# Scores of windowed attention on four quarters of the array, and value rows loaded with padding to 128 partitions

## The chip, the cores and the metric

The kernel runs on one core of a Trainium2 chip. Its engines work side by side: TensorE (PE in the profile, its weight loads PEld), VectorE (DVE), ScalarE (ACT), GpSimd (POOL) and SyncE (SP), which here only issues transfers. Transfers are carried by 16 DMA engines. The metric is the device time of one execution in microseconds (us); lower is better.

## The reference

Three stages follow one another: windowed attention, a routed mixture of experts with a skip score, and a second mixture of experts that fills each expert up to a capacity. The change is in the first one only:

```python
B, H, S, D = q.shape                       # 4, 8, 768, 64
block, window = (32, 16)
k_sum = k.reshape(B, H, nb, block, D).max(axis=3)     # nb = 24 block keys
v_sum = v.reshape(B, H, nb, block, D).mean(axis=3)    # 24 block values
scores_l = scale * np.matmul(q, k.transpose(0, 1, 3, 2))
mask_l = np.abs(pos[:, None] - pos[None, :]) < window
scores_s = scale * np.einsum('bhsd,bhnd->bhsn', q, k_sum) + np.log(block)
a = softmax(concat(where(mask_l, scores_l, -1e9), scores_s))
out = a @ concat(v, v_sum)
```

## The kernel before, in words

`phase_a` computes the attention and the gate logits of the first mixture. A *unit* is one batch and four heads (8 units, numbered 0 to 7); each unit is done in six *steps*, 48 in all. A step has four pairs of a head pair `h` and a window `w` of 64 queries; from unit 1 on these are two head pairs times the two windows 2t and 2t+1. A window sees 118 keys: 24 block keys and 94 neighbours. Queries and keys hold the 64 dims of two heads on the two halves of the 128 partitions.

Loop `i` runs over the steps, and the engines carry out their work in the order in which it is written there. In loop `i` TensorE gets:

- `qk(i)`, the scores: for each of the four pairs and each half `r` of the partitions, a product of 64 rows by 64 columns by 118 keys, written to the same half `r` of the PSUM tile `s_ps`. In float32 each product is two instructions of the trace, so 16 a step (L122). VectorE adds the mask and takes the maximum (L126).
- `ptr(i-2)`, four transposes (L137) of the exponentials that ScalarE made in loop `i-1` (`ex`, L132). ScalarE copies the result out (L139) ahead of the next `ex`.
- `pv(i-3)`, the products with the value rows (L148), 16 instructions: 118 rows by 64 columns by 65 (64 values and a column of ones for the sum). VectorE divides (L150 to L156).
- in the loops that follow odd units, `logits` (L172 to L177) and `post` (L162, L164): the gate's products and the transposes of the finished rows. The text calls these *post steps*.

So one step's scores run in the loop in which older steps are transposed and multiplied. The even window reads its keys from `kt`, the odd one from the copy `K2`, both of which ScalarE completes (L100, L103, L104) from the block maxima that VectorE takes (`prep_k`, L96).

Value rows: tile `VV` has, for each of the 12 windows, 24 rows of block means on partitions 0 to 23 and 96 rows of values on partitions 24 to 119. The values come by two DMAs a unit (L86) of 96 partitions; the ones of the mean rows are written once (L66). The means are made from a second copy of the values, `vt` (L84): POOL adds them up (`add_v`, L109), TensorE turns them (`turn_v`, L111), ScalarE scales them (L114), and POOL copies them into rows 0 to 23 (`mean_v`, L115). There are three `VV` tiles, used in turn.

`load(u)` issues a unit's transfers on the one SP queue, in this order: keys and queries of head pair 0, of head pair 1, `vt`, and the two of `VV`. Units 0 and 1 are issued at the start, unit `u+2` in the third step of unit `u`. SP waits where a buffer or a semaphore isn't free yet, and everything behind it waits too.

PSUM has eight banks: `s_ps`, `pt_ps` and `o_ps` with two buffers each, `xt_ps` and `l_ps` with one each.

After `phase_a` come the two mixtures, whose first weights are issued when the most loaded expert is known (late in `phase_a`).

Of the kernel before, what the change touches and what calls it, by code (L numbers as in the profile page):

```python
# [6 lines left out]
F32=mybir.dt.float32; BF=mybir.dt.bfloat16; F32R=mybir.dt.float32r; I32=mybir.dt.int32; U32=mybir.dt.uint32  # L7
AF=mybir.ActivationFunctionType; OP=mybir.AluOpType; AX=mybir.AxisListType
PSUM=bass.MemoryType.PSUM
B,H,S,D=4,8,768,64  # L10
N=B*S; DM=512; E=8; F=1024; CAP=384
NT=6
# [11 lines left out]
def layout(inp):  # L24
    q,k,v=inp['q'],inp['k'],inp['v']
    qd=np.ascontiguousarray(q.reshape(B,4,2,S,D).transpose(0,2,4,1,3)).reshape(B,128,4,S)
    kd=np.ascontiguousarray(k.reshape(B,4,2,S,D).transpose(0,2,4,1,3)).reshape(B,128,4,S)
    vd=np.ones((B,2,VR,4,65),np.float32)
    vd[:,:,:15]=0; vd[:,:,15+S:]=0
    vd[:,:,15:15+S,:,:64]=v.reshape(B,2,4,S,D).transpose(0,1,3,2,4)  # L30

    vd=vd.reshape(B,2,VR,260)[:,:,np.arange(VP)[:,None]+64*np.arange(12)[None,:]].reshape(B,2,VP,4,780)
    vd=np.concatenate([vd,np.zeros((B,2,VP,4,4),np.float32)],4)
    w17=np.concatenate([inp['moe_w_skip'][:,None],inp['moe_w_gate'],inp['moe2_w_gate']],1)
    w17=w17.reshape(4,128,17).transpose(1,0,2).reshape(128,68)
    w17=np.concatenate([w17,np.zeros((128,15),np.float32)],1)

    j=np.arange(94)[None,:]; c=np.arange(128)[:,None]%64
    band=(j>=c)&(j<=c+30)
    m=np.zeros((3,128,118),np.float32)  # L40
    m[:,:,:24]=np.float32(8*np.log(32))
    ok=[band&(j>=15), band, band&(j<=78)]
    for i in range(3): m[i,:,24:]=np.where(ok[i],0.0,NEG)
    cst=np.concatenate([m.transpose(1,0,2).reshape(128,354),np.eye(128,dtype=np.float32)],1).astype(np.float32)
    vt=np.ascontiguousarray(v.reshape(B,2,2,2,24,32,D).transpose(0,3,6,1,5,2,4)).reshape(B,128,2,1536)
    return dict(q=qd,k=kd,v65=vd,vt=vt,w17=w17,cst=np.ascontiguousarray(cst))

def phase_a(nc,tc,ctx,I,st):
    V=nc.vector; A=nc.scalar; T=nc.tensor; G=nc.gpsimd
    cl=ExitStack(); ld=cl.enter_context(tc.tile_pool(name="a_ld",bufs=2,side="right"))  # L50
    cp=ctx.enter_context(tc.tile_pool(name="a_const",bufs=1))
    wk=ctx.enter_context(tc.tile_pool(name="a_wk",bufs=3))
    ps=ctx.enter_context(tc.tile_pool(name="a_ps",bufs=2,space=PSUM))
# [3 lines left out]
    VV=[]; K2=[cp.tile([128,2,NT,118],F32,name=f"K2_{i}") for i in range(2)]  # L57

    wm=K2[1][:,0].rearrange("p a b->p (a b)")[:,0:256]; V.memset(wm,1.0); wm=wm.bitcast(BF)
    def spin(k,wm=wm):  # L60
        p=ps.tile([128,4,128],F32,name="s_ps").rearrange("p a b->p (a b)")
        for _ in range(k): T.matmul(p,wm[:,0:128] if len(wm.shape)==2 else wm[:,0,0:128],wm,start=True,stop=True)
    spin(WARM)
    for i in range(3):
        t=cp.tile([24+VP,12,4,65],F32,name=f"VV_{i}")
        G.memset(t[0:24,:,:,64:65],1.0); VV.append(t)  # L66
    KT=[]
    for i in range(3):
        t=ld.tile([128,2,864],F32,name=f"kt{i}",bufs=1)[:,:,25:25+KW]
# [7 lines left out]
    def load(u):  # L77
        b,g=units[u]
        kt=KT[u%3]; qd=ld.tile([128,2,S],F32,name="qd",bufs=3); vt=st["raw"].tile([128,2048],F32,name="wraw")
        vv=VV[u%3]; src=I['v65']  # L80
        def ld_k(h0,h1): nc.sync.dma_start(kt[:,h0:h1,39:39+S],I['k'][b,:,2*g+h0:2*g+h1,:])
        def ld_q(h0,h1): nc.sync.dma_start(qd[:,h0:h1],I['q'][b,:,2*g+h0:2*g+h1,:])
        def ld_v():
            nc.sync.dma_start(vt[:,0:1536],I['vt'][b,:,g])  # L84
        def ld_vv():
            for s0 in (0,2): nc.sync.dma_start(vv[24:24+VP,3*s0:3*s0+6].rearrange("p (a s) h d -> p a (s h d)",s=3),src[b,g,:,s0:s0+2,0:780])  # L86
        U[u]=dict(kt=kt,qd=qd,vt=vt,vv=vv,k2=K2[u%2])
        U[u]['ks']=wk.tile([128,2,24],F32,name="ks",bufs=2)
        ld_k(0,1); ld_q(0,1)
        if u==0: nc.sync.dma_start(cst,I['cst'])  # L90
        ld_k(1,2); ld_q(1,2); ld_v(); ld_vv()
        if u==0: nc.sync.dma_start(w17,I['w17'])
# [23 lines left out]
    X={}; XT={}; D={}  # L116
    def qk(i):
        u,pairs=steps[i]; d=U[u]
        p=ps.tile([128,4,128],F32,name="s_ps")
        for j,(h,w) in enumerate(pairs):  # L120
            for r in (0,64):
                T.matmul(p[r:r+64,j,0:118],d['qd'][r:r+64,h,64*w:64*w+64],d['k2'][r:r+64,h,w//2,:] if w%2 else d['kt'][r:r+64,h,64*w:64*w+118],start=True,stop=True)  # L122
        sb=wk.tile([128,4,118],F32,name="s_sb"); nm=wk.tile([128,4],F32,name="nm")
        for j,(h,w) in enumerate(pairs):
            mk=mask[:,0 if w==0 else (2 if w==11 else 1),:]
            V.tensor_tensor_reduce(out=sb[:,j,:],in0=p[:,j,0:118],in1=mk,scale=-0.125,scalar=3e38,op0=OP.add,op1=OP.min,accum_out=nm[:,j:j+1])  # L126
        D['sb',i]=(sb,nm)
    def ex(i):
        sb,nm=D.pop(('sb',i))
# [11 lines left out]
    def pv(i):  # L141
        u,pairs=steps[i]; d=U[u]; b,g=units[u]
        pts=D.pop(('pt',i))
        o=ps.tile([128,4,128],F32,name="o_ps")

        for j0,e,j in [(j0,e,j) for j0 in (0,2) for e in range(2) for j in (j0,j0+1)]:
            h,w=pairs[j]; r=64*(w%2); k=2*(h if u else w//2%2)+e
            T.matmul(o[r:r+64,k,0:65],pts[:,j,64*e:64*e+64],d['vv'][0:118,w,2*h+e,:],start=True,stop=True)  # L148
        rs=wk.tile([128,4],F32,name="rs"); rc=wk.tile([128,4],F32,name="rc")
        V.tensor_scalar(rs,o[:,:,64],1e-9,None,op0=OP.add)  # L150
        V.reciprocal(rc,rs)
        if b not in X:
            X[b]=(cp if b%2 else ld).tile([128,NT,ROW],F32,name=f"X{b%2}",bufs=1)
            G.memset(X[b][:,:,512:ROW],0.0)
        h,w=pairs[0]; t=w//2
        if u: V.tensor_mul(X[b][:,t,256*g:256*g+256].rearrange("p (h d)->p h d",d=64),o[:,:,0:64],rc[:,:,None].to_broadcast([128,4,64]))  # L156
        else:
            for j in range(2): V.tensor_mul(X[b][:,t+j,128*h:128*h+128].rearrange("p (h d)->p h d",d=64),o[:,2*j:2*j+2,0:64],rc[:,2*j:2*j+2,None].to_broadcast([128,2,64]))
    def post(b,t):
        x=X[b][:,t,:]  # L160
        p=ps.tile([128,4,128],F32,name="xt_ps",bufs=1)
        for k in range(4): T.transpose(p[:,k,:],x[:,128*k:128*k+128],ident)  # L162
        XT[b,t]=wk.tile([128,4,128],F32,name="xT",bufs=2)
        A.copy(XT[b,t],p)  # L164
    def logits(i):


        now,old=tile(i),tile(i-1)
        if not (now or old or i+PL+1 in AT_M): return
        l=ps.tile([128,4,128],F32,name="o_ps") if old==(B-1,NT-1) else ps.tile([128,4,128],F32,name="l_ps",bufs=1)  # L170
        if now:
            for k in range(4): T.matmul(l[32*k:32*k+32,0,:],w17[:,17*k:17*k+32],XT[now][:,k,:],start=True,stop=True)  # L172
        if old: T.transpose(l[:,1,:],XT.pop(old)[:,0,:],ident)
        if i+PL+1 in AT_M: turn_v(AT_M[i+PL+1],l)
        if now: A.copy(XT[now][:,0,:],l[:,0,:])
        if i+PL+1 in AT_M: mean_v(AT_M[i+PL+1],l)
        if old: V.tensor_reduce(st['lg'][:,old[0]*NT+old[1],:],l[:,1,:].rearrange("p (k j)->p j k",k=4)[:,0:17],AX.X,OP.add)  # L177
    def tile(j):

        return (steps[j][0]//2,j%NT) if 0<=j<n and steps[j][0]%2==1 else None  # L180
    def group(b,t):
        return (3,b*NT) if b==B-1 and t==2 else (6,b*NT) if b<B-1 and t==5 else None
    def gate1(b,t):
        if group(b,t):
            n,c=group(b,t)
            l1=st['lg'][:,c:c+n,1:9]
            m=wk.tile([128,6],F32,name="g_m",bufs=2)[:,0:n]; V.tensor_reduce(m,l1,AX.X,OP.max)
            d=wk.tile([128,6,8],F32,name="g_d",bufs=2)[:,0:n]; V.tensor_tensor(d,l1,m[:,:,None].to_broadcast([128,n,8]),op=OP.subtract)
            A.activation(d,d,AF.Exp)
            r=st['route1'].group(c,n,m,lambda:ps.tile([128,4,128],F32,name="s_ps").rearrange("p a c->p (a c)") if b==B-1 else ps.tile([128,512],F32,name="l_ps",bufs=1)); next(r)  # L190
            D['gd',c]=d,r
    def gate2(b,t):
        if group(b,t):
# [17 lines left out]

    def first1(b,t):
        if t==5:
            D['first']=st['route1'].first(lambda:ps.tile([128,4,128],F32,name="s_ps").rearrange("p a c->p (a c)")); next(D['first']); st['raw0']()
    def first2(b,t):
        if t==5: next(D['first'])
    def first3(b,t):
# [6 lines left out]
    n=len(steps)  # L224
# [4 lines left out]
    for i in range(n+PL+3):  # L229
        u,t=(i//NT,i%NT)  # L230
# [17 lines left out]
        for lag in range(10):  # L248
            j=i-PL-1-lag
# [3 lines left out]
        if i<n and u and u+1<8:  # L253

            s=SHIFT1 if u==1 else SHIFT
# [7 lines left out]
        if i==9: nc.sync.dma_start(st['xrows'][0:128,:].rearrange("p (a c)->p a c",c=129),zr[:,None,:].to_broadcast([128,4,129])); st['load_const']()  # L263
        if i==15: st['const']()
        for s in splits.get(i-n,()): st['split'](*s)
        if i in (n+1,n+2): st['warm'](ps.tile([128,4,128],F32,name="s_ps").rearrange("p a c->p (a c)"),2)
        if i==n+2: x0=ps.tile([128,4,128],F32,name="s_ps"); st['xT0'](x0,0)
        if i==n+3: st['xT0'](x0,1)

    nc.sync.dma_start(st['xrows'][128+128*(NCOL-3):,0:DM].rearrange("(t p) d -> p t d",p=128),X[B-1][:,3:6,0:DM])  # L270
# [862 lines left out]
```

## Time and profile before

| | |
|---|---|
| runs | 649.26 us median of 3 (646.45 to 651.44) |
| profiled execution | 653.37 us, of which 651.6 us are the span shown in the profile |
| busy in the span | PE 595.5 us (91%), PEld 478.1 (73%), DVE 428.8 (66%), ACT 328.7 (50%), POOL 364.0 (56%) |
| scores, L122 | 768 instructions, 38.9 + 36.5 us busy |
| VV loads, L86 | 16 of 585.0 KB, median 16.9 us from issue to landing |
| vt loads, L84 | 8 of 768.0 KB |

The first score starts at 6.7 us and the last group of scores at 148.6 us; the mixtures take the rest. A busy share says how long an engine had an instruction in it, not that it set the pace; for that one reads the chain of work that ended last and what each wait ended on. Matmuls overlap, so a matmul's own duration is longer than the distance to the next one.

### The profile page before, as it was taken

The numbers are of one execution on the slowest core, as the hardware profiler recorded it, in microseconds if no ns is written. First come the engines' busy times: TensorE is split into PE (matmuls) and PEld (weight loads), VectorE is DVE, ScalarE is ACT, GpSimd is POOL, SyncE is SP. The second block draws the span as 40 slices with busy tenths as digits, with TensorE's granted clock in tenths as the row PEclk, the third lists the DMA queues.
The fourth block names the chain that finished last, engine by engine and source line by source line (L and its number), as shares of the span: only waits on it lengthen the run. The fifth ranks groups of instructions, "written<-read, shape, count | busy, mean of one in ns | idle before, by whom it ended". The sixth has DMA issues, their size and how long they took to land.

```text
span 651.6 us, 13438 instructions
## 1 busy us (share of the span) xinstructions
PE 595.5 (91%) x4848; PEld 478.1 (73%) x4848; DVE 428.8 (66%) x1618; ACT 328.7 (50%) x740; POOL 364.0 (56%) x404
## 2 busy tenths in 40 slices
PE   8789899988799999995389979999999999999994
PEld 4567677766588777773268768797888979798983
DVE  4657879688778899665766647667776766742110
ACT  5678788768337667720053243452626354263610
POOL 2454464622354787760075375693939579397931
PEclk9999899989789999998589989999999999999997
DMA  8998979437239966600260812609063360854000
GB/s 253 302 272 241 281 242 288 131 118 273 98 115 375 307 226 232 203 17 10 88 220 1 308 49 87 253 18 325 31 252 105 124 216 21 323 190 163 33 17 33
DMA packets 47620, 111.43 MB, mean 171 GB/s; under 512 B 3937, under 2 KB 4705, under 8 KB 47552
## 3 DMA queue, kind: packets, MB, share of 16 engines
q1 hardware_dynamic: 38992, 85.41, 40.6%
q0 software_dynamic: 6208, 20.39, 9.0%
q10 hardware_dynamic: 2352, 4.76, 2.0%
q8 instruction: 39, 0.64, 0.4%
q14 instruction: 29, 0.24, 0.1%
HBM read 96.07 MB, written 14.88 MB: 170 GB/s over the span
## 4 chain that ended last, share of the span: by engine, by line
PE 63%; DVE 13%; DMA 8%; issue 7%; POOL 5%; ACT 2%; POOLq 0%; SPq 0%; DVEq 0%; ACTq 0%
PE dh_ps L961 7%; PE dh_ps L962 6%; PE dh_ps L963 6%; PE dz_ps L978 5%; PE dz_ps L980 5%; PE dz_ps L979 5%; PE s_ps L122 4%; DMA qd<-in_q_dram 3%; DMA wraw<-in_vt_dram 3%; PE pt_ps L137 3%; PE o_ps L148 3%; DVE wl L503 3%; POOL wl L932 2%; PE z_ps L588 2%; PE z_ps L589 1%
## 5 line engine op out<-in xcount | busy, mean ns | idle before, releaser
L932 POOL TENSOR_TENSOR wl<-wraw,wh 128x512 fp32r<-128x512 f32 x124 | 155.5, 1288 | 9.9 <-ACT wh L923 9.5
L961 PE MATMUL dh_ps<-dxh,wh 128*128 128x384 f32 x256 | 92.5, 361 | 2.1 <-ACT dxh L953 2.1
L962 PE MATMUL dh_ps<-dxl,wh 128*128 128x384 f32 x256 | 88.5, 346 | 0.6 <-DVE dxl L953 0.6
L963 PE MATMUL dh_ps<-dxh,wl 128*128 128x384 f32 x256 | 87.8, 343 | 0.0
L978 PE MATMUL dz_ps<-wh,dhh 128*128 128x512 f32 x192 | 78.9, 411 | 0.0
L980 PE MATMUL dz_ps<-wh,dhl 128*128 128x512 f32 x192 | 76.0, 396 | 0.0
L979 PE MATMUL dz_ps<-wl,dhh 128*128 128x512 f32 x192 | 76.0, 396 | 0.0
L923 ACT CAST wh<-wraw 128x512 fp32r<-128x512 f32 x128 | 73.5, 619 | 2.8 <-DMA wraw<-in_w1b_dram 2.8
L985 POOL DMA_INDIRECT out_dram<-dz,io x24 | 24.5, 1022 | 86.9 <-ACT dz L983 84.8
L966 ACT ACTIVATE dhh<-dh_ps 128x384 fp32r<-128x384 f32 x64 | 31.4, 491 | 80.5 <-PE dh_ps L963 69.6
L967 DVE SCALAR_TENSOR_TENSOR dhl<-dh_ps,dhh 128x384 fp32r<-128x384 f32 x64 | 35.5, 555 | 54.5 <-ACT dhh L966 54.5
L132 ACT ACTIVATE p_e<-s_sb,nm 128x118 f32<-128x118 f32 x192 | 59.7, 386 | 0.4 <-DVE nm L126 0.4
L983 ACT COPY dz<-dz_ps 128x512 f32<-128x512 f32 x24 | 14.1, 587 | 85.4 <-PE dz_ps L980 60.3
L503 POOL TENSOR_TENSOR wl<-wraw,wh 128x1024 fp32r<-128x1024 f32 (+1 forms) x18 | 37.4, 2105 | 27.5 <-ACT wh L502 27.5
L961 PEld LDWEIGHTS dh_ps<-dxh,wh 128*128 128x128 f32 x256 | 49.2, 192 | 2.7 <-ACT dxh L953 2.4
L962 PEld LDWEIGHTS dh_ps<-dxl,wh 128*128 128x128 f32 x256 | 49.3, 192 | 2.4 <-DVE dxl L953 2.4
L502 ACT CAST wh<-wraw 128x1024 fp32r<-128x1024 f32 (+1 forms) x56 | 49.0, 933 | 4.0 <-DMA wraw<-in_w1a_dram 3.7
L126 DVE CUSTOM_DVE_ANT_0 s_sb<-s_ps,cst 128x118 f32<-128x118 f32 x192 | 41.8, 274 | 12.8 <-PE s_ps L122 10.8
L109 POOL TENSOR_TENSOR wraw<-wraw 128x384 f32<-128x384 f32 (+4 forms) x39 | 30.8, 789 | 34.7 <-DMA wraw<-in_vt_dram 20.5
L963 PEld LDWEIGHTS dh_ps<-dxh,wl 128*128 128x128 f32 x256 | 49.0, 192 | 0.0
L503 DVE TENSOR_TENSOR wl<-wraw,wh 128x1024 fp32r<-128x1024 f32 (+1 forms) x38 | 45.0, 1221 | 4.5 <-ACT wh L502 4.4
L115 POOL COPY VV<-wraw 24x1024 f32<-24x1024 f32 x24 | 24.0, 1031 | 37.5 <-ACT wraw L114 37.5
(344 smaller groups left out, 1373.0 us busy)
## 6 DMA issues: line engine op xcount, KB each, us to landing
wraw<-in_w1b_dram SPq DMA_DIRECT2D x16, 1024.0 KB, 6.1
wraw<-in_w2b_dram SPq DMA_DIRECT2D x14, 1024.0 KB
wraw<-in_w2a_dram SPq DMA_DIRECT2D x12, 1024.0 KB, 8.5
wraw<-in_w1a_dram SPq DMA_DIRECT2D x10, 1024.0 KB
VV<-in_v_dram SPq DMA_DIRECT2D x16, 585.0 KB, 16.9
kt<-in_k_dram SPq DMA_DIRECT2D x16, 384.0 KB, 9.7
qd<-in_q_dram SPq DMA_DIRECT2D x16, 384.0 KB, 6.8
wraw<-in_vt_dram SPq DMA_DIRECT2D x8, 768.0 KB, 14.0
```

Of the source, the lines that this page charges most:

```text
L126: V.tensor_tensor_reduce(out=sb[:,j,:],in0=p[:,j,0:118],in1=mk,scale=-0.125,scalar=3e38,op0=OP.add,op1=OP.min,accum_out=nm[:,j:j+1])
L132: A.activation(pe[:,j,:],sb[:,j,:],AF.Exp,bias=nm[:,j:j+1],scale=-1.0)
L502: (hi.tensor_copy if hi else nc.scalar.copy)(h[:,c],t[:,c])
L503: (lo or nc.vector).tensor_tensor(l[:,c],t[:,c],h[:,c].bitcast(F32),op=OP.subtract)
L923: A.copy(h[:,c],t[:,c])
L932: eng.tensor_tensor(l[:,c],t[:,c],h[:,c].bitcast(F32),op=OP.subtract)
L961: T.matmul(q,wh[:,c],s['xh'][:,d,:],start=(d==0),stop=False)
L962: T.matmul(q,wh[:,c],s['xl'][:,d,:],start=False,stop=False)
L963: T.matmul(q,wl[:,c],s['xh'][:,d,:],start=False,stop=(d==3))
L978: T.matmul(q,s['hh'][:,f,c0],wh[:,c],start=(f==0),stop=False)
L979: T.matmul(q,s['hh'][:,f,c0],wl[:,c],start=False,stop=False)
L980: T.matmul(q,s['hl'][:,f,c0],wh[:,c],start=False,stop=(f==7))
```

## The change

The scores of a step go to two PSUM tiles, `s0_ps` for the first head of each pair and `s1_ps` for the second. A product's input half is given by the head (`e`), its output half by the window's parity (`y`), so that four successive products use the four different quarters of the array, where before they used two quarters on the diagonal. The products, their sizes and their number stay. The order of the rows in the softmax tile changes with it (the two halves of the partitions are now the two windows), and the mask and the products with the values are indexed to match; in the latter two successive instructions still use the two halves of the columns.

Two banks are needed for the second score tile: `xt_ps` now takes its turns in `pt_ps`, and `l_ps` in `o_ps`.

The value rows are laid out with 24 rows ahead (zeros, with ones in the 65th columns) and 8 rows of zeros behind, so that each DMA fills all 128 partitions of `VV`, 780 KB in place of 585 KB. The memsets of the ones (L66) go. The means are copied into rows 0 to 23 as before, but now into rows that the DMA also writes.

```diff
-    vd=np.concatenate([vd,np.zeros((B,2,VP,4,4),np.float32)],4)
+    vd=np.concatenate([np.zeros((B,2,24,4,780),np.float32),vd,np.zeros((B,2,8,4,780),np.float32)],2)
+    vd[:,:,0:24,:,64::65]=1; vd=np.concatenate([vd,np.zeros((B,2,128,4,4),np.float32)],4)
...
-    ok=[band&(j>=15), band, band&(j<=78)]
+    ok=[band&((j>=15)|~lo), band, band&((j<=78)|lo)]
...
-        t=cp.tile([24+VP,12,4,65],F32,name=f"VV_{i}")
-        G.memset(t[0:24,:,:,64:65],1.0); VV.append(t)
+        VV.append(cp.tile([128,12,4,65],F32,name=f"VV_{i}"))
...
-            for s0 in (0,2): nc.sync.dma_start(vv[24:24+VP,3*s0:3*s0+6].rearrange("p (a s) h d -> p a (s h d)",s=3),src[b,g,:,s0:s0+2,0:780])
+            for s0 in (0,2): nc.sync.dma_start(vv[:,3*s0:3*s0+6].rearrange("p (a s) h d -> p a (s h d)",s=3),src[b,g,:,s0:s0+2,0:780])
...
-        p=ps.tile([128,4,128],F32,name="s_ps")
-        for j,(h,w) in enumerate(pairs):
-            for r in (0,64):
-                T.matmul(p[r:r+64,j,0:118],d['qd'][r:r+64,h,64*w:64*w+64],d['k2'][r:r+64,h,w//2,:] if w%2 else d['kt'][r:r+64,h,64*w:64*w+118],start=True,stop=True)
+        p=[ps.tile([128,4,128],F32,name=f"s{e}_ps") for e in range(2)]
+        for x in range(2):
+            for e,y in ((0,0),(1,1),(0,1),(1,0)):
+                h,w=pairs[2*x+y]; r=slice(64*e,64*e+64)
+                T.matmul(p[e][64*y:64*y+64,x,0:118],d['qd'][r,h,64*w:64*w+64],d['k2'][r,h,w//2,:] if y else d['kt'][r,h,64*w:64*w+118],start=True,stop=True)
         sb=wk.tile([128,4,118],F32,name="s_sb"); nm=wk.tile([128,4],F32,name="nm")
-        for j,(h,w) in enumerate(pairs):
-            mk=mask[:,0 if w==0 else (2 if w==11 else 1),:]
-            V.tensor_tensor_reduce(out=sb[:,j,:],in0=p[:,j,0:118],in1=mk,scale=-0.125,scalar=3e38,op0=OP.add,op1=OP.min,accum_out=nm[:,j:j+1])
+        for j in range(4):
+            t=pairs[j//2*2][1]//2; mk=mask[:,0 if t==0 else (2 if t==NT-1 else 1),:]
+            V.tensor_tensor_reduce(out=sb[:,j,:],in0=p[j%2][:,j//2,0:118],in1=mk,scale=-0.125,scalar=3e38,op0=OP.add,op1=OP.min,accum_out=nm[:,j:j+1])
...
-        for j0,e,j in [(j0,e,j) for j0 in (0,2) for e in range(2) for j in (j0,j0+1)]:
-            h,w=pairs[j]; r=64*(w%2); k=2*(h if u else w//2%2)+e
-            T.matmul(o[r:r+64,k,0:65],pts[:,j,64*e:64*e+64],d['vv'][0:118,w,2*h+e,:],start=True,stop=True)
+        for k in range(4):
+            for y in range(2):
+                h,w=pairs[k//2*2+y]; r=slice(64*y,64*y+64)
+                T.matmul(o[r,k,0:65],pts[:,k,r],d['vv'][0:118,w,2*h+k%2,:],start=True,stop=True)
...
-        p=ps.tile([128,4,128],F32,name="xt_ps",bufs=1)
+        p=ps.tile([128,4,128],F32,name="pt_ps")
...
-        l=ps.tile([128,4,128],F32,name="o_ps") if old==(B-1,NT-1) else ps.tile([128,4,128],F32,name="l_ps",bufs=1)
+        l=ps.tile([128,4,128],F32,name="o_ps")
```

## Rows read from the trace of the kernel before

**Rows 1.** Busy times by stretch: stretch, length, engines with instruction counts, PEclk, DMA share, GB/s.

```profile
6.50:46.50 40.00, 30.78 (x447) 22.82 (x447) 23.89 (x146) 27.46 (x83) 16.47 (x21) 1.00 1.03 287
46.50:61.00 14.50, 14.50 (x229) 11.15 (x228) 9.91 (x59) 12.03 (x37) 7.13 (x9) 1.00 0.91 230
61.00:75.50 14.50, 12.65 (x200) 10.02 (x196) 13.69 (x70) 11.94 (x37) 9.39 (x21) 0.98 0.98 285
```

**Rows 2.** PE timeline, start and length: where it waited up to 46.5 us.

```profile
19.11 0.69 PE L148 MATMUL o_ps<-VV,pt_sb 118*64 118x65 f32 x16 [0.92 <-POOL VV L115]
...
31.14 0.39 PE L111 MATMUL l_ps<-cst,wraw 128*24 128x128 f32 x2 [1.83 <-POOL wraw L109]
...
41.06 0.42 PE L122 MATMUL s_ps<-kt,qd 64*64 64x118 f32 x4 [0.89 <-ACT kt L103]
...
45.77 0.39 PE L111 MATMUL l_ps<-cst,wraw 128*24 128x128 f32 x2 [2.27 <-POOL wraw L109]
```

**Rows 3.** Chain that ended last, start and length: a load, then a post step.

```profile
22.46 18.80 DMA wraw<-in_vt_dram
...
49.81 0.95 PE s_ps L122 x16
50.76 0.58 PE pt_ps L137 x4
51.34 0.61 PE o_ps L148 x16
51.96 0.36 PE l_ps L172 x8
52.31 0.26 PE l_ps L173
52.57 0.44 PE xt_ps L162 x4
53.01 0.95 PE s_ps L122 x16
```

**Rows 4.** The same chain in unit 5, a step without post, and VectorE's stretch.

```profile
70.26 1.80 DVE r_cand L342
...
102.79 0.95 PE s_ps L122 x16
103.74 0.58 PE pt_ps L137 x4
104.33 0.62 PE o_ps L148 x16
104.94 0.95 PE s_ps L122 x16
```

**Rows 5.** ACT timeline in unit 0, start and length, idle before in brackets.

```profile
11.70 0.58 ACT L139 COPY pt_sb<-pt_ps 118x512 f32<-118x512 f32 x1 [0.42 <-PE pt_ps L137]
12.18 1.25 ACT L132 ACTIVATE p_e<-s_sb,nm 128x118 f32<-128x118 f32 x4
13.85 0.59 ACT L139 COPY pt_sb<-pt_ps 118x512 f32<-118x512 f32 x1 [0.42 <-PE pt_ps L137]
```

**Rows 6.** Stretches in which mostly one kind of load ran; columns as Rows 1.

```profile
10.50:14.00 3.50, 3.49 (x30) 2.13 (x32) 1.95 (x14) 2.67 (x9) 0.28 (x1) 1.00 1.04 228
66.50:70.00 3.50, 3.50 (x61) 2.83 (x59) 3.25 (x17) 3.07 (x10) 1.51 (x2) 1.00 1.04 211
18.00:20.00 2.00, 1.08 (x20) 0.82 (x19) 1.48 (x9) 1.77 (x6) 1.97 (x2) 1.00 1.09 434
147.00:155.00 8.00, 8.00 (x127) 6.17 (x125) 7.00 (x39) 7.55 (x23) 3.47 (x7) 1.00 1.04 390
```

**Rows 7.** All engines in a post step of unit 4, start and length.

```profile
84.93 0.58 ACT L139 COPY pt_sb<-pt_ps 118x512 f32<-118x512 f32 x1 [0.76 <-PE pt_ps L137]
...
85.97 0.43 DVE L156 TENSOR_TENSOR X<-o_ps,rc 128x256 f32<-128x256 f32 x1
...
86.70 0.59 ACT L164 COPY xT<-xt_ps 128x512 f32<-128x512 f32 x1
...
87.45 0.66 PE L137 MATMUL pt_ps<-cst,p_e 128*118 128x128 f32 x4
```

**Rows 8.** POOL timeline, start and length: the first copies of means.

```profile
18.03 3.00 POOL L115 COPY VV<-wraw 24x1024 f32<-24x1024 f32 x3 [1.82 <-ACT wraw L114]
```

**Rows 9.** Chain that ended last after a pause of PE, at the lower clock.

```profile
75.57 1.77 PE s_ps L122 x16
77.34 1.03 PE pt_ps L137 x4
```

More of the change, by code (lines that the diff above doesn't have):

```diff
@@ L36, in layout @@
     w17=np.concatenate([w17,np.zeros((128,15),np.float32)],1)
-    j=np.arange(94)[None,:]; c=np.arange(128)[:,None]%64
+    j=np.arange(94)[None,:]; c=np.arange(128)[:,None]%64; lo=np.arange(128)[:,None]<64
     band=(j>=c)&(j<=c+30)
@@ L60, in spin @@
     def spin(k,wm=wm):
-        p=ps.tile([128,4,128],F32,name="s_ps").rearrange("p a b->p (a b)")
+        p=ps.tile([128,4,128],F32,name="s0_ps").rearrange("p a b->p (a b)")
         for _ in range(k): T.matmul(p,wm[:,0:128] if len(wm.shape)==2 else wm[:,0,0:128],wm,start=True,stop=True)
@@ L189, in gate1 @@
             A.activation(d,d,AF.Exp)
-            r=st['route1'].group(c,n,m,lambda:ps.tile([128,4,128],F32,name="s_ps").rearrange("p a c->p (a c)") if b==B-1 else ps.tile([128,512],F32,name="l_ps",bufs=1)); next(r)
+            r=st['route1'].group(c,n,m,lambda:ps.tile([128,4,128],F32,name="s0_ps" if b==B-1 else "o_ps").rearrange("p a c->p (a c)")); next(r)
             D['gd',c]=d,r
@@ L213, in first1 @@
         if t==5:
-            D['first']=st['route1'].first(lambda:ps.tile([128,4,128],F32,name="s_ps").rearrange("p a c->p (a c)")); next(D['first']); st['raw0']()
+            D['first']=st['route1'].first(lambda:ps.tile([128,4,128],F32,name="s0_ps").rearrange("p a c->p (a c)")); next(D['first']); st['raw0']()
     def first2(b,t):
@@ L265, in phase_a @@
         for s in splits.get(i-n,()): st['split'](*s)
-        if i in (n+1,n+2): st['warm'](ps.tile([128,4,128],F32,name="s_ps").rearrange("p a c->p (a c)"),2)
-        if i==n+2: x0=ps.tile([128,4,128],F32,name="s_ps"); st['xT0'](x0,0)
+        if i in (n+1,n+2): st['warm'](ps.tile([128,4,128],F32,name="s0_ps").rearrange("p a c->p (a c)"),2)
+        if i==n+2: x0=ps.tile([128,4,128],F32,name="s0_ps"); st['xT0'](x0,0)
         if i==n+3: st['xT0'](x0,1)
```

## Prediction

> **What bounds the kernel now.** The change lies in the attention, the first 150 us of 653, so I first took the table of stretches. Up to 46.5 us the DMA engines are full (share 1.03) while PE is busy 30.8 us of 40; from there PE is busy nearly all the time and DMA a little less than always [rows 1]. So there are two stages. In the first, step 12 and those before it wait for loads: PE pauses of 1.83 and 2.27 us end on POOL's sums, which start when `vt` has landed (18.8 us after its issue), 0.89 us on keys, 0.92 us on means [rows 2, 3]. In the second, from step 13 at 46.6 us on, I read the chain that ended last. In a post step it runs through PE alone: scores 0.95, transposes 0.58, values 0.61, gate 0.36 and 0.26, post 0.44, then the next scores, 3.20 us in all [rows 3]. A step without post is 0.95 + 0.58 + 0.62 = 2.15 us, again all PE [rows 4]. Between 61.0 and 75.5 us VectorE is busy 13.7 us of 14.5 [rows 1]; its operations of the routing, one stretched to 1.80 us [rows 4], lie on the chain there, and PE pauses.
>
> **A score step on four quarters.** The four transposes of `post` take 0.44 us, 110 ns for one instruction of 128 columns that has the array to itself; one of 118 columns would be 101 ns. The 16 of the scores take 0.95 us [rows 3], and eight times 101 ns is 0.81: the two quarters on the diagonal run side by side today, and 0.14 is the start. That four can run at once is shown for four strips of columns: the gate's eight instructions of 128 columns take 0.36 us [rows 3], where one after another they would take 0.88. Two by two quarters isn't in the trace. Its bounds: no overlap beyond today's, 0.95; four at a time, 0.14 + 4 × 0.101 = 0.55. I take 0.55, since strips and halves both overlap: 0.40 us off every score step.
> [...]
>
> **What a shorter score step is worth.** In post steps PE has no pause, ScalarE does (0.76 us ahead of L139 [rows 7]), so 3.20 becomes 2.80. In steps without post another circle takes over: copy of the transposes, exponentials, the last transpose, copy again. In unit 0, where PE has no value products yet, it went round in 13.85 - 11.70 = 2.15 us with ScalarE waiting 0.42 us for PE [rows 5]. That is what such a step takes today, so the 0.40 us are worth nothing there; PE then waits 0.40 us more for exponentials.
> From step 13 on I count 13 post steps that PE paces (the rest stand under VectorE): 5.2 us. Three steps with gate but no post go from 2.76 to 2.36 (1.2), three with one gate transpose from 2.41 to 2.15 (0.8), three with the turning of means (0.3 to 0.4 us of PE) to 2.15 (0.9). Two steps that ran at the lower clock after a pause, scores 1.77 us [rows 9], give 0.8 each (1.6). Together 9.7. Against it: ScalarE's copies of keys fall into some post steps and pass 2.80 us there, 0.7 in all; and 2 us I take off because the stretches on VectorE have no slack to hand on the gain, and the last steps also split weights whose transfer starts when routing is done, not when PE is. Second stage: 7 us, bounds 2 and 10.
>
> **The value loads.** Each grows from 585 to 780 KB. Two stretches in which nearly only VV moved show 228 and 211 GB/s at a full DMA share; keys and queries, and the weights, all of 128 partitions, show 434 and 390 [rows 6]. All are contiguous rows of a few KB, so what sets VV apart is 96 partitions from 24 on (or its rows of 3,120 bytes). One VV load is today 599 kB / 0.220 = 2.7 us of a full DMA. With 128 partitions at 390 to 434 GB/s it is 799 kB / 0.41 = 1.95; if the low rate stays, 3.6. I take 2.0, nearer the rows of the same shape: 0.7 us less for each of 16, and whatever is queued behind them starts earlier.
> [...]
>
> **The first stage.** On the one queue up to `vt` of unit 2 lie three units' keys, queries and `vt` (3 × 2,304 KB), four VV loads and 0.3 MB of constants: with the padding 10.5 MB, 26 us at 0.40 MB/us. With 3 us of start and landing it lands near 29, not at 41.3 us; POOL's 4.5 us of sums then end near 34. Step 13 could start at 35 by the loads. PE and ScalarE need more: from 46.6 I take the pauses on loads (1.83 + 0.89 + 2.27 = 5.0 us [rows 2]) and 0.40 for each of steps 8 to 12 that PE paces (2.0), which gives 39.6. The pause of 0.92 us and the steps of unit 0 I leave, since the circle on ScalarE paces them. First stage: 7 us, bounds 3 and 10.
>
> **Edits costed at nothing.** The means' copies (L115) must now wait for the VV loads. A unit is issued ten steps before its means are copied, over 21 us, against 16.9 us of landing today. For unit 0 the copy starts at 18.0 us [rows 8]; its loads end near 14. If they came at the old rate it would wait until about 20, 2 us. `xt_ps` in `pt_ps`: a transpose then waits for the copy one allocation back instead of two; L139 ends at 85.5 and L164 at 87.3, the next transposes into that bank start at 87.4 and after 88.5 [rows 7], so there is 1 us even after the 0.40 are gone. `l_ps` in `o_ps`: VectorE's division ends at 86.4 [rows 7], the next value products start 1.6 us later. Uncovered, either would cost some tenths in each of some 24 post steps, up to 4 us. Mask, order of the value products and the missing memsets change no instruction's size; the second bank for the scores adds no wait.
>
> **Sum.** 653.4 - 7 - 7 = 639.4 for the profiled execution, which is 4.1 above the median of the runs. From 649.3: **635 us**.
>
> **Rivals.**
> - *The quarters don't overlap by fours* (12%). Score steps stay 0.95; only the loads' pauses go: -5, **644 us**. For it: no such pattern in the trace. Against it: strips of columns do.
> - *VV takes as long as before* (10%). The first stage gives only PE's 2 us: 649.3 - 2 - 7 = **640 us**. [...] Against: 434 beside 228 GB/s.
> - *Both happen, ScalarE and VectorE eat it* (14%). If key copies, shared banks and routing leave 2 us of the second stage: 649.3 - 7 - 2 = **640 us**. For it: ScalarE busy 12.0 of 14.5 us [rows 1].
> - *The low rate belongs to the rows of 3,120 bytes* (6%). Then VV takes 3.6 us: four loads ahead of `vt` of unit 2 cost 3.6 us, PE's share gives 1 back; later a pair of units brings four VV, 3.6 us more for a DMA that is already at 0.91 to 0.98 [rows 1], so the second stage gains nothing: 649.3 + 2.6 = **652 us**, slower. It decides once VV's rate stays under some 290 GB/s, where 799 kB take 2.7 us.
> - *The clock* (4%). After the pause in VectorE's stretch (PE busy 12.7 of 14.5 us) transposes ran 1.03 us in place of 0.58 [rows 1, 9]. If pauses of 0.4 us a step did this too, some 17 steps without post would cost 1 us more each: 635 + 17 + the lost gain, about **655**. [...]
>
> **Chances and range.** My forecast (both parts, 629 to 641) has 54%. 627 to 645 takes in the next three rivals and leaves out the last two and some beyond either end. A measurement here can tell about 1%, 6.5 us, from nothing. Under 642.8: the forecast, most of the 640s and a third of the 644, 0.76; within 1%: 0.17; slower: 0.07.
>
> **What would show it.** Right: 16 scores in some 0.55 us on the chain; VV stretches near 400 GB/s; pauses on L109 gone and step 13 near 39 us; post steps of 2.8 us and others still 2.15 with PE waiting on `p_e`; end of scores near 134 us. Wrong: scores at 0.95 (first rival); VV still 220 GB/s; PE waiting for `xT`, `X` or means; a granted clock well under 1 from 40 to 130 us.

## The result, and the profile after

The changed kernel took 640.95 us (median of 4 runs, 637.4 to 643.8) beside 648.34 us for the kernel before in the same comparison: ratio 0.9888, 95% interval 0.9849 to 0.9926. Two repetitions gave 0.9898 (0.9867 to 0.9929) and 0.9862 (0.9819 to 0.9905). By these ratios it is faster by 1.0 to 1.4%, 6.6 to 8.9 us; forecast were 14 us, 635. The time lies in the range, the gain is about half of the forecast. Runs more than 1.5% above the fastest of the same kernel count as slow, and the ratios, as well as the medians in the tables below, leave them out.

The first trace of the changed kernel (643.75 us, span 642.1), the busy times by stretch, the columns as in [rows 1] and the stretches laid at its own step 13:

```profile
6.50:42.70 36.20, 28.16 (x447) 19.84 (x447) 23.86 (x146) 27.02 (x81) 16.48 (x21) 0.95 1.03 403
42.70:57.20 14.50, 14.50 (x253) 10.33 (x253) 11.13 (x66) 13.25 (x42) 9.35 (x22) 1.00 1.03 364
57.20:71.70 14.50, 13.81 (x241) 9.82 (x241) 13.74 (x84) 13.62 (x41) 7.05 (x8) 1.00 0.82 307
```

The loads move at 403 GB/s in the first stage where 287 stood [rows 1] (a part of the bytes is padding), and step 13 starts at 42.8 us, not 46.5. The PE timeline of a post step, start and length:

```profile
45.58 0.31 PE L123 MATMUL s_ps<-kt,qd 64*64 64x118 f32 x1
45.59 0.32 PE L123 MATMUL s_ps<-K,qd 64*64 64x118 f32 x2
45.60 0.39 PE L123 MATMUL s_ps<-kt,qd 64*64 64x118 f32 x2
45.74 0.27 PE L123 MATMUL s_ps<-K,qd 64*64 64x118 f32 x2
45.75 0.34 PE L123 MATMUL s_ps<-kt,qd 64*64 64x118 f32 x2
45.84 0.27 PE L123 MATMUL s_ps<-K,qd 64*64 64x118 f32 x2
45.85 0.34 PE L123 MATMUL s_ps<-kt,qd 64*64 64x118 f32 x2
45.94 0.27 PE L123 MATMUL s_ps<-K,qd 64*64 64x118 f32 x2
45.95 0.26 PE L123 MATMUL s_ps<-kt,qd 64*64 64x118 f32 x1
46.14 0.65 PE L138 MATMUL pt_ps<-cst,p_e 128*118 128x128 f32 x4
46.73 0.69 PE L150 MATMUL o_ps<-VV,pt_sb 118*64 118x65 f32 x16
47.34 0.43 PE L174 MATMUL o_ps<-xT,w 128*32 128x128 f32 x8
47.70 0.33 PE L175 MATMUL o_ps<-cst,xT 128*128 128x128 f32 x1
47.87 0.60 PE L164 MATMUL pt_ps<-cst,X 128*128 128x128 f32 x4
48.40 0.31 PE L123 MATMUL s_ps<-kt,qd 64*64 64x118 f32 x1
```

After the first, the instructions of the scores (two for each product) start in fours, 0.10 us apart (45.74, 45.84, 45.94), and the transposes follow 0.56 us after the first score, where 0.95 stood [rows 3]: the four quarters run side by side. The step takes 48.40 - 45.58 = 2.82 us, where 3.20 stood [rows 3].

PE's waits up to step 13, by what ended them: total, times, longest. None is on POOL's sums (L109) any more; keys cost 3.4 us and means 2.1.

```profile
PE s_ps L123 <- ACT kt L103: 3.4, 2, 1.9
PE o_ps L150 <- POOL VV L115: 2.1, 2, 1.0
PE pt_ps L138 <- ACT p_e L133: 2.0, 4, 1.1
```

### The profile page after: what moved, and what is told of

The parts are those of the page before. It is cut to its first block, busy times and chain, and to the rows that moved or that the text cites. A ratio compares the mean times of both kernels' runs of the same rounds, so it can differ in the third digit from the quotient of the medians.

```text
span 642.1 us, 13487 instructions
## 1 busy us (share of the span) xinstructions
PE 588.6 (92%) x4848; PEld 465.5 (73%) x4848; DVE 426.4 (66%) x1618; ACT 328.0 (51%) x740; POOL 364.9 (57%) x401
## 4 chain that ended last, share of the span: by engine, by line
PE 40%; issue 5%; POOL 3%; DVE 3%; DMA 1%; ACT 1%; POOLq 0%; DVEq 0%; ACTq 0%
PE dh_ps L963 7%; PE dh_ps L964 7%; PE dh_ps L965 6%; PE dz_ps L980 5%; PE dz_ps L982 5%; PE dz_ps L981 5%; POOL wl L934 2%; PE dh_ps L952 2%; DMA xg<-xrows,p_ix 1%; PE rt_ps L810 1%; POOL out_dram L987 1%; DVE p_g L801 1%; PE rt_ps L808 1%; ACT dxh L955 0%; ACT wh L925 0%
## 5 line engine op out<-in xcount | busy, mean ns | idle before, releaser
L963 PE MATMUL dh_ps<-dxh,wh 128*128 128x384 f32 x256 | 94.2, 368 | 2.5 <-ACT dxh L955 2.5
L964 PE MATMUL dh_ps<-dxl,wh 128*128 128x384 f32 x256 | 89.8, 351 | 0.4 <-DVE dxl L955 0.3
L504 ACT CAST wh<-wraw 128x1024 fp32r<-128x1024 f32 (+1 forms) x56 | 48.9, 932 | 6.3 <-DMA wraw<-in_w1a_dram 6.0
L941 POOL DMA_INDIRECT xg<-xrows,p_ix x24 | 23.3, 973 | 38.5 <-DVE rrow L875 24.3
```

The source lines that it names most:

```text
L504: (hi.tensor_copy if hi else nc.scalar.copy)(h[:,c],t[:,c])
L963: T.matmul(q,wh[:,c],s['xh'][:,d,:],start=(d==0),stop=False)
L964: T.matmul(q,wh[:,c],s['xl'][:,d,:],start=False,stop=False)
```

## The experiments

### Each half alone, and both kernels again

`scores_only` is the changed kernel with the value rows as before, so it has the shared banks too; `values_only` is the kernel before with only the padded rows. `after_again`, `after_third` and `before_again` are the two kernels, unchanged.

```diff
 scores_only, against the changed kernel
...
-        VV.append(cp.tile([128,12,4,65],F32,name=f"VV_{i}"))
+        t=cp.tile([24+VP,12,4,65],F32,name=f"VV_{i}")
+        G.memset(t[0:24,:,:,64:65],1.0); VV.append(t)
...
-            for s0 in (0,2): nc.sync.dma_start(vv[:,3*s0:3*s0+6]...
+            for s0 in (0,2): nc.sync.dma_start(vv[24:24+VP,3*s0:3*s0+6]...
 values_only, against the kernel before: the same lines the other way round
```

> The change without the padded value rows: scores on four quarters, VV loaded as 96 partitions from 24 on. If the shorter score steps carry the second stage (my theory), score steps take 0.55 us, VV stays near 220 GB/s, step 13 starts near 46 us as before, the last scores start at 148.6 - 8 to 11 = 138 to 141 us. If the earlier value loads carry most (rival: what changed VectorE's stretch and the pauses on POOL is the load), the last scores start near 146. Total, set against the kernel before: -8 to -10 us by the first at an equal clock, -2 by the second.

> The kernel before with only the value rows padded to 128 partitions: scores on the diagonal, 0.95 us a step. Theory: VV at 400 GB/s, the pauses on POOL's sums (1.83 + 2.27 us) go, step 13 starts at 42.8 to 44 us, and later steps keep 3.20 and 2.15 us; VectorE's stretch loses 1 to 2 us, since the routing's operation r_cand no longer runs beside POOL's late sums (0.71 in place of 1.79 us); last scores start at 143 to 145 us. Rival (loads are hidden but for the first stage): 146 or later. Total -3 to -5 us against the kernel before, or -2 by the rival.

> The changed kernel once more, for a second trace and more times. Last scores start at 133.5 us again (within 0.5). Question: is the 5.4 us that the mixtures took longer in the first trace the change's, or the clock's of that execution? If the clock wanders by itself, the mean granted clock differs from 0.946 and the time less half of the low-clock time, (1 - clock) x span / 2, comes again to 624 to 626 us; if the change brings it, the routing stretch from 283 to 314 us is at 0.50 again and the total stays 640 to 644.

> The kernel before once more, for a second trace. Last scores start at 148.6 us again (within 0.5). If the clock wanders by itself, the low stretches of the mixtures (303.5 to 327.4 us in the first trace) lie or last otherwise here, and the time less half of the low-clock time is 639 to 640 us again; if the mixtures' clock is the program's own, the low stretches lie where they lay, within 2 us.

### The attention stage alone

The six microseconds between the two profiled executions of the kernel before (653.4, 652.8 us) and the median of its other runs (647.2) had to be placed. So the four versions also ran without the mixtures:

```diff
-            with ExitStack() as c2: phase_b(nc,tc,c2,I,st,W)
...
-        phase_d(nc,tc,ctx,I,st,out,R,W,wk,ps,cp)
...
+    nc.sync.dma_start(st['out'][0:128,:],X[B-1][:,5,0:DM])
```

> The attention stage of the kernel before alone: both mixtures are left out, and 128 rows of the result are written instead. Open: two profiled executions of the kernel before took 653.4 and 652.8 us, while the median of its many other runs is 647.2. If the 96-partition loads make the attention's length vary (theory), the times here spread over 4 to 8 us, the profiled execution is at the upper end (last scores near 148.5 us) and the median some 5 us under it. If the 6 us lie in the mixtures (rival), all runs here agree within 1.5 us.

> The attention stage of the changed kernel alone, mixtures left out as in the kernel beside it. Loads no longer bind, so by the theory its runs agree within 2 us, and its median is 9 to 11 us under that of the attention of the kernel before; by the rival it is 14.5 to 15 us under it, as the two traces have it (133.5 against 148.6), and the rest is given back by the mixtures.

> The attention stage with scores on four quarters and value rows of 96 partitions, mixtures left out. Traces: last scores at 144.4 us, 4.2 us less than before. By the theory (loads vary) the times spread as those of the kernel before, and the median is 5 to 7 us under its median; by the rival 4 us, with 1.5 us of spread.

> The attention stage with scores on the diagonal and value rows of 128 partitions, mixtures left out. Trace: last scores at 140.8 us, 7.7 us less than before. By the theory the runs agree within 2 us and the median is only 2 to 3 us under that of the attention of the kernel before; by the rival 7.5 us under it.

### What the four versions gave

From the traces, one figure for each execution that was profiled (whole kernel and attention alone), in us:

| | step 13 starts | last scores start | between |
|---|---|---|---|
| before | 46.5, 48.9, 45.9 | 148.6, 148.2, 147.9 | 102.0, 99.2, 101.9 |
| values alone | 42.8, 42.7 | 140.8, 140.8 | 98.1, 98.1 |
| scores alone | 45.9, 47.4 | 144.4, 143.2 | 98.5, 95.8 |
| both | 42.8, 43.2, 44.4, 44.8 | 133.5, 134.0, 134.3, 136.2 | 90.7, 90.8, 89.9, 91.5 |

From the times, with the median granted clock; in brackets the lowest and highest time, and how many of the runs are counted:

| | whole kernel, median | clock | ratio, interval | attention alone, median | clock |
|---|---|---|---|---|---|
| before | 647.2 (641.9 to 652.3, 62 of 66) | 0.961 | | 168.3 (168.2 to 169.4, 3 of 5) | 0.960 |
| values alone | 645.8 (641.1 to 647.5, 12 of 12) | 0.959 | 0.9997 (0.9968 to 1.0025) | 164.3 (164.0 to 164.7, 4 of 5) | 0.978 |
| scores alone | 643.7 (637.8 to 645.6, 8 of 12) | 0.949 | 0.9946 (0.9907 to 0.9984) | 160.5 (1 of 4) | 0.955 |
| both | 640.2 (636.7 to 643.8, 21 of 21) | 0.952 | 0.9888 to 0.9862, above | 160.6 (159.0 to 161.2, 4 of 4) | 0.918 |

In the traces the two halves help each other. Alone, the padded rows bring the last scores forward by 7.4 us (means of the rows: 148.2 to 140.8) and the quarters by 4.4; together it is 13.7. With fast loads the score steps give 6.3. With slow loads they give less: in `att_scores` TensorE still waits on POOL's sums, which stand behind the loads, for 3.2 us; in `att_values` no such wait is left, and its three longest are others (total, times, longest):

```profile
PE o_ps L111 <- POOL wraw L109: 3.2, 2, 2.5
```

```profile
PE s_ps L122 <- ACT kt L103: 2.6, 2, 1.7
PE l_ps L347 <- DVE r_oh L344: 2.1, 1, 2.1
PE o_ps L148 <- POOL VV L115: 1.7, 2, 1.0
```

My theory for `scores_only` (8 to 11 us earlier) was too high, and these waits are a likely reason. For `values_only` both the theory (143 to 145 us) and the rival (hidden loads, 146 or later) were too late: 140.8 came.

The times tell less, and they do not agree with the traces. By the profiled executions the padded rows alone are worth 8.0 us (645.3 against 653.4), and both halves 13.4 (mean of three, 639.7, against 653.1 of two). By the ratios of the runs the padded rows alone can't be told from nothing, the quarters alone give 3.5 us, and both 6.6 to 8.9; the 3 to 5 us expected of the padded rows, and the 8 to 10 expected of the quarters, did not come. In the attention alone the padded rows give 4.0 us between the medians (expected 2 to 3, by the rival 7.5) and both halves 7.7 (expected 9 to 11, or 14.5 to 15); one run is too little to judge the quarters by.

My theory was that the kernel before varies with its 96-partition loads and that its traces show it on the long side. The runs do not show it. The spread of 4 to 8 us that I expected of the attention alone came, 6.5 us over five runs, but two long runs make it and the other three agree within 1.2; with padded rows, too, one run of five lies 3.1 us above the next. The three traces with the old loads and diagonal scores agree on the last scores within 0.7 us (148.6, 148.2, 147.9), although the value rows took 41.6, 45.0 and 42.6 us in them. What is plain is that both profiled executions of the kernel before lie high among its runs: only three of the 65 others took longer than 652.8 us. In fact all five profiled executions with the old loads lie above the median of their kernel's runs, by 3.5 us and more, but of eight with padded rows only three; so it isn't excluded either that being profiled costs time with the old loads. No trace of one of the shorter executions was taken, and the cause of these 6 us stays open.

What the traces do show of the loads: the 96-partition rows took 41.2, 41.4, 41.6, 42.6 and 45.0 us of all 16 DMA engines (sum of the single transfers over 16) in five executions; 128-partition rows, a third more bytes, 32.8 to 33.2 us in eight others. Steps 22 and 23, where VectorE's routing stands, took 9.6, 6.6 and 9.6 us in the three traces with the old loads and diagonal scores, 6.7 and 9.9 with the old loads and quarters, and 6.5 to 6.6 in all eight with padded rows.

### The first stage, and the clock

Busy times over the first 36.2 us, of `values_only`, of `after_again` and of the attention alone with both changes; the third figure from the end is the granted clock:

```profile
6.50:42.70 36.20, 30.69 (x447) 22.93 (x447) 23.95 (x146) 27.07 (x82) 16.46 (x21) 1.00 1.03 401
```

```profile
6.50:42.70 36.20, 29.26 (x444) 20.85 (x445) 23.92 (x146) 26.49 (x79) 16.44 (x21) 0.86 1.03 402
```

```profile
6.50:42.70 36.20, 29.00 (x437) 20.77 (x440) 23.10 (x144) 26.54 (x80) 16.43 (x21) 0.84 1.03 407
```

With padded rows and diagonal scores PE was busy for 30.7 us and the clock stayed at 1.00 (also in the two other traces with these scores and loads). With the quarters PE was busy for 28.2 to 29.3 us, waited for ScalarE instead, and the clock came to 0.84 to 0.95 in four traces. In the first trace of the changed kernel a stretch at the lower level, a granted clock of 0.50, runs from 23.7 to 27.1 us; it begins where PE starts again after a wait of 1.92 us on keys:

```profile
23.67 0.43 PE L123 MATMUL s_ps<-kt,qd 64*64 64x118 f32 x1 [1.92 <-ACT kt L103]
```

The quarters are not the only way to such a fall: the kernel before, with its waits on loads, stood at 1.00, 0.91 and 0.95 in its three traces over the same 36.2 us. Step 13 starts at 42.7 to 42.8 us with padded rows alone and at 42.8 to 44.8 with the quarters added: in this stage they gave nothing, and cost up to 2 us.

Later there is the same price. In the first trace of the changed kernel TensorE stood still for 1.35 and 1.84 us between the first two experts of the second mixture, the clock fell at 365.1 us, between the two pauses, and what followed ran at 0.50 for 13.6 us:

```profile
363.92 0.66 PE L952 MATMUL dh_ps<-cb,xg 128*128 128x128 f32 x4 [1.35 <-DMA xg<-xrows,p_ix]
...
368.79 0.69 PE L963 MATMUL dh_ps<-dxh,wh 128*128 128x384 f32 x1 [1.84 <-ACT dxh L955]
```

```profile
345.00:365.00 20.00, 18.65 (x124) 14.10 (x122) 11.28 (x46) 5.19 (x10) 7.95 (x11) 1.00 0.76 277
365.00:378.70 13.70, 11.82 (x50) 10.34 (x49) 6.33 (x18) 3.99 (x9) 8.42 (x7) 0.50 0.06 20
```

In `after_again` that stretch was short:

```profile
366.50:369.90 3.40, 3.40 (x11) 3.40 (x12) 1.00 (x2) 0.00 (x0) 3.40 (x4) 0.50 0.00 0
```

The two executions, 643.75 and 638.25 us, differ by 5.5 us. Behind the same instructions the difference is 1.0 us at 300 us, 2.5 at 342, and 5.5 at 436 and to the end; 2.9 us of it arise in the stretch above, and 2.0 in an earlier one that ran at the lower level (0.50) for 6.8 us instead of 3.4. In the first pair of traces the last scores start 15.1 us earlier and the span is only 9.5 us shorter; so these 5.6 us that the mixtures gave back weren't the change's own, but mostly the clock's of that execution. In the kernel before it wanders too: its longest stretch at the lower level (0.50) ran from 303.5 to 327.4 us in the first trace and from 296.8 to 327.5 in `before_again`. I had expected that the time less half of the low-clock time is the same each time. It held only roughly for the changed kernel (621.7 to 626.4 us) and not for the kernel before (631.2 to 640.0 in `before_again`, where 639 to 640 was expected). A share is systematic: the changed kernel spends 61 us at the lower level in its median run, the kernel before 50 (estimated as twice 1 - clock, times the span, since the first traces of both kernels show a granted clock of either 1.00 or 0.50). A line through the 21 and the 62 runs gives 0.22 and 0.31 us of time for each of them; 10 us more are 2 to 3.5 us, an estimate.

### Idle products in the pauses

```diff
-            except StopIteration: cur=None
+            except StopIteration: 
+                cur=None
+                if curp==0: warm(nc,st,R.psum(),5)
...
+                if q==1: warm(nc,st,R.psum(),6)
                 curp=q; cur=expert(q); npc=0; continue
```

> The changed kernel with 11 idle products on TensorE (bf16, 512 columns) between the first and the second expert of the second mixture: 5 where it waits for the gathered rows (1.2 to 2.0 us in the traces), 6 where it waits for their high halves (1.4 to 1.8 us). Theory: these two pauses are why the granted clock falls to 0.50 right behind them (13.6 us long in the first trace of the changed kernel, 3.4 in the second, 3.4 and 6.8 in those of the kernel before), which costs half of each such stretch. With the pauses filled the clock stays at 1.00 there and the kernel gains 1.7 to 5 us against the changed kernel in the same call: 636 to 638. Rival: the clock falls whatever stands in these pauses, or the fillers delay the work by as much: no gain, or up to 1 us lost.

> The changed kernel beside the one with idle products: 640 us, last scores at 133.5 to 136 us, a mean granted clock of 0.944 to 0.965, and a stretch of 0.50 of 3.4 to 13.6 us behind the first expert.

Median 641.2 us (10 runs) against 637.6 (6 runs): no gain. Nor is a loss told by it, for the three sets of runs of the changed kernel have medians of 641.0, 640.2 and 637.6. The fillers didn't land where they were meant to. PE timeline of `after_warm`, in brackets the idle time ahead:

```profile
359.39 0.66 PE L952 MATMUL dh_ps<-cb,xg 128*128 128x128 f32 x4 [1.36 <-DMA xg<-xrows,p_ix]
...
362.06 0.61 PE L489 MATMUL rt_ps<-it,ones_b 128*128 128x512 bf16 x1 [0.95 <-DVE p_e L821]
...
366.77 0.59 PE L489 MATMUL rt_ps<-it,ones_b 128*128 128x512 bf16 x2 [1.56 <-DVE p_thr L826]
...
367.88 0.53 PE L963 MATMUL dh_ps<-dxh,wh 128*128 128x384 f32 x1
```

They stand behind the first pause, and wait for a PSUM bank that VectorE still reads, 0.95 and 1.56 us, with the rest of TensorE's queue behind them. From the first product on the gathered rows to the second expert's first product it took 8.5 us (359.39 to 367.88), where the three other traces of the changed kernel have 4.4 to 4.9. So these fillers, in a shared bank, came with 3.6 to 4.1 us more there. A stretch at 0.50 came all the same, from 361.6 us on and 3.4 us long; whether pauses that are really filled would hold the clock stays open.

### Shared banks

```diff
...
-        p=ps.tile([128,4,128],F32,name="xt_ps",bufs=1)
+        p=ps.tile([128,4,128],F32,name="pt_ps")
...
-        l=ps.tile([128,4,128],F32,name="o_ps") if old==(B-1,NT-1) else ps.tile([128,4,128],F32,name="l_ps",bufs=1)
+        l=ps.tile([128,4,128],F32,name="o_ps")
...
```

> The attention stage alone, scores on the diagonal, value rows of 128 partitions, and only the sharing of banks added: xt_ps in pt_ps, l_ps in o_ps (the mixtures are left out). My prediction costs the sharing at nothing: median 164.5 us as without it (164.0 to 164.7 but for one run), within 0.5. If it costs some tenths in each of 24 post steps (its bound): 166 to 168.5.

164.7 us (163.9 to 166.1, 4 runs) against 164.3 without the sharing: within the 0.5 us that were expected, and nothing that can be told. In its one trace the last scores start 1.5 us later than in `att_values` (142.2 and 140.7 us), of which a longer stretch at the lower clock near 132 us (6.8 us in place of 3.4) is the larger part.

### Value rows to other ranges of partitions

```diff
-            for s0 in (0,2): nc.sync.dma_start(vv[:,3*s0:3*s0+6]...
+            c=slice(*{3:(0,96),4:(32,128),5:(24,120),6:(0,64),7:(16,112)}.get(u,(0,128)))
+            for s0 in (0,2): nc.sync.dma_start(vv[c,3*s0:3*s0+6]...
```

> The attention stage of the changed kernel alone (mixtures left out), with the value rows of units 3 to 7 loaded to other ranges of partitions, so that rows are missing or old there: 0 to 95, 32 to 127, 24 to 119, 0 to 63 and 16 to 111; units 0 to 2 load all 128. A transfer of one row (3,120 bytes) took 124 ns with 128 partitions and 187 to 271 ns with 24 to 119. If the number of partitions sets it, every range of 96 is slow (200 ns and more). If the start at 24 sets it, 0 to 95 and 32 to 127 take 125 to 135 ns and 24 to 119 stays over 200.

Stretches of 2 us with mostly value rows, in this order: all 128 partitions (with keys), 0 to 95, 32 to 127, 24 to 119, 0 to 63, 16 to 111; the last two columns are DMA share and GB/s.

```profile
32.00:34.00 2.00, 1.58 (x36) 1.36 (x36) 1.25 (x10) 1.71 (x6) 2.00 (x3) 1.00 1.03 404
40.00:42.00 2.00, 2.00 (x35) 1.55 (x36) 1.00 (x9) 0.90 (x3) 0.00 (x0) 0.94 1.01 218
56.00:58.00 2.00, 2.00 (x37) 1.47 (x37) 1.36 (x12) 2.00 (x9) 0.00 (x0) 1.00 0.98 210
69.00:71.00 2.00, 1.63 (x29) 1.31 (x29) 1.90 (x13) 1.86 (x7) 0.00 (x0) 1.00 0.93 218
87.00:89.00 2.00, 1.48 (x23) 1.00 (x19) 1.32 (x5) 2.00 (x8) 0.01 (x1) 1.00 1.02 201
97.00:99.00 2.00, 2.00 (x38) 1.43 (x36) 1.86 (x4) 2.00 (x7) 1.91 (x2) 1.00 1.01 239
```

One transfer of 3,120 bytes took 124 to 126 ns in the median of the three units with 128 partitions, 213, 241, 221, 247 and 204 ns in the others. So it is neither the start at 24 nor the row's length: all five ranges short of 128 that were tried are slow.

## Why the prediction was half right

- **Score step, 0.40 us** [rows 3, 5]: right, 0.56 us measured; post steps 2.82 for 2.80, steps without post 2.13 to 2.14 us for 2.15. The rival without overlap fell.
- **Second stage, 7 us from the score steps**: right in size where the loads are fast. From step 13 to the last scores `values_only` took 98.1 us and the changed kernel 90.7, 7.4 less. With the old loads it is 3.9 (means of the table, 101.0 to 97.2).
- **Value loads, 2.7 to 2.0 us** [rows 6]: right; 392 to 407 GB/s in stretches of mostly value rows, and the rivals of slow loads fell. But the sum gave the loads nothing in the second stage. There they brought 4.0 us in the first traces (102.0 to 98.1; 1.1 against the second trace, 99.2), for part of VectorE's stretch [rows 4] was loads too: steps 22 and 23 went from 9.6 us to 6.6.
- **First stage, 7 us**: mis-sized, 3.8 (46.5 to 42.8), all from the loads. The 2.0 us for shorter steps 8 to 12 didn't come: keys and means, both behind ScalarE, bound next, as the waits above show. The two failed terms nearly cancel in the traces, which is luck: 3.8 in the first stage and 11.3 in the second are 15.1 us, forecast 7 and 7.
- **"From 649.3: 635"**: the step that failed. It took a gain read in one execution off the median of others, as if the 4.1 us between them were a constant. Between profiled executions the gain did come, 13.4 us (653.1 to 639.7, means of two and three), and the 639.4 us forecast for the profiled execution is near that mean; but the changed kernel's profiled executions lie around its median (640.2), and the kernel before's lie 6 us above its own (647.2). By the runs the gain is 7 us. Why the profiled executions of the kernel before are long isn't shown; that its removed pauses are shorter in its other runs is one reading, a cost of profiling the old loads another.
- **The clock, a rival of 4%**: partly right. It did not fall in the steps without post (1.00 from 42.7 to 71.7 us, and in the first trace on to 126), but behind pauses such as the 1.92 us on keys in the first stage. It cost 2 to 3.5 us by the estimate above, a part of what is missing. Not every pause brings the fall: in the first trace of the kernel before PE paused 9 of 40 us in the first stage and the clock stayed at 1.00 [rows 1], while two others with its scores and loads show 0.91 and 0.95 there.
- **ScalarE and VectorE eat it** (640 us) met the time by another way: its 2 us of second stage were 7.4.
- **Edits at nothing**: right for the banks. Copies of means wait longer, 2.1 us in two pauses for 0.92 [rows 2]; the padded rows alone show 1.7, so most of this comes with them.

## What to carry over

Take a predicted gain off the execution it was read in, and ask whether that execution is a typical one before you take it off the median: here the profiled one was longer than nearly all other runs. Ask it of waits on transfers above all: steps 22 and 23 took 6.6 to 9.9 us with the old loads, while a post step took 2.81 to 2.82 in every trace with quarters at the full clock. A shorter step on one engine is worth its length only where no load and no other engine's circle ends at the same time; measure the two halves of a change alone and together. When an engine's work shrinks and it then waits, look at its granted clock before counting the gain.

## What the runs showed of the hardware

Loads to fewer than 128 partitions ran at 201 to 239 GB/s in the five ranges tried, where 128 partitions had 404. Loads beside them were slow too: transfers of 3,072 bytes took 244 to 252 ns beside rows to 32 to 127 and 252 beside rows to 0 to 63, and 122 to 125 beside rows to all 128. Why is not shown.

Three operations of VectorE's routing lasted about as long as a sum of POOL beside them. In `att_scores` an operation of the routing that takes 0.64 us in the changed kernel took 1.72; the DVE timelines of the changed kernel and of `att_scores`, and the POOL timeline of the latter:

```profile
65.36 0.64 DVE L345 TENSOR_TENSOR r_oh<-r_cand,r_do 128x48 bf16<-128x48 f32 x1
```

```profile
71.23 1.72 DVE L346 TENSOR_TENSOR r_oh<-r_cand,r_do 128x48 bf16<-128x48 f32 x1
```

```profile
71.07 4.02 POOL L109 TENSOR_TENSOR wraw<-wraw 128x768 f32<-128x768 f32 x4 [2.27 <-DMA wraw<-in_vt_dram]
```

The first of these POOL sums began at 71.07 us. In the kernel before, a sum of this size took 1.81 us (70.17 to 71.98), so this one ended near 72.88, an estimate; VectorE's operation, begun 0.16 us after its start, ended at 72.95. The 1.80 us in [rows 4] has the same pattern: VectorE's operation, 1.78 us from 70.26 in its timeline, ended 0.06 us behind POOL's sum. With the 0.64 us of the changed kernel it is the same on a smaller scale: beside it POOL has a shorter sum, of 0.60 us from 65.34, and the operation ended 0.06 us behind that one too. In `att_scores` the operation of the same size just ahead, begun before POOL's sum, took 0.21 us. In these three traces the length of VectorE's operation went with the POOL sum it met (1.8 us in `att_scores` and in the kernel before, 0.60 in the changed kernel); in the first two the sum starts after a wait on `vt` (2.27 us in `att_scores`, 2.16 in the kernel before), and so when that load has landed. Why is not shown.

```profile
65.34 0.60 POOL L109 TENSOR_TENSOR wraw<-wraw 128x192 f32<-128x192 f32 x1
```

```profile
70.99 0.21 DVE L345 TENSOR_TENSOR r_cand<-r_cand,r_mx 128x48 f32<-128x48 f32 x1
```
